# Retention and a gated FFN on one core: where the transposes of q and k, one unit's norm and the last output product stand

## The chip, the cores and the metric

The kernel runs on one core of one Trainium2 chip. The metric is the device time of one execution in microseconds (us), as a median of several runs. The core has five engines with an instruction queue each: TensorE (PE in the profile; PEld is its weight load), VectorE (DVE), ScalarE (ACT), GpSimd (POOL) and SyncE (SP), which here only issues transfers. Each engine takes its instructions in the order in which the program gives them, and waits on semaphores for the others.

## The reference

Retention over 8 batches, 8 heads, 576 positions and head size 64, followed by an RMS norm and a gated feed-forward net over the 4608 tokens that result:

```python
scores = scale * np.matmul(q, k.transpose(0, 1, 3, 2))
Dmat = np.where(rel >= 0, gamma[:, None, None] ** rel[None, :, :], 0.0)
attn = np.matmul(scores * Dmat[None], v)            # (8, 8, 576, 64)
x = attn.transpose(0, 2, 1, 3).reshape(4608, 512)
xn = x / np.sqrt(np.mean(x * x, -1, keepdims=True) + 1e-6) * rms_g
g = xn @ w_gate                                     # 512 -> 1536
out = (g * (1.0 / (1.0 + np.exp(-g))) * (xn @ w_val)) @ w_out   # 1536 -> 512
```

Everything is computed in fp32. The weights arrive as 64-bit floats and are turned into fp32 on the device, at the start.

## The kernel before

The 4608 tokens are cut into 12 *units* of 384 tokens (NU = 12, U = 384). The attention is cut into 32 *jobs* of one batch and two heads each. Units 0 and 1 are computed plainly in `start()`, while the weights are still being converted; `down(u, s)` there computes three blocks of 128 rows of a unit's output, and each copies its sums out on ACT. Between these blocks `start()` also puts the norm of unit 2 (`norm_0`: squares on ACT and their sums on DVE; `norm_1`: the mean by three small products on PE, the power -0.5 on POOL; `diagonals`; `norm_2`: one product `rb` on PE, then four scalings of `x` and four differences into `x` and `sums` on DVE), the attention's jobs 8 and 9 (`slot`), and `combine(1)`, which makes sums of blocks of `w_val` on POOL.

From unit 2 on, the two up-projections and the output projection are each done as a 2x2 block product with seven products in place of eight. Its sums of blocks are made on DVE.

`up(u, m, g)` is one *group*: m = 0 is the gate, m = 1 the value, g one of three pairs of columns. A unit has six groups, i = 0 to 5, with m = i % 2. One group is seven products of four matmuls into four PSUM banks x, y, z, w. Each bank is named for the tile, and a later product of the same group adds to it. The order, with the readers, is:

1. A11 into x; ACT copies x to `m`.
2. S2 into y; DVE: u = m + y (written `u<-m,y`).
3. S1 into z; DVE: u4 = u + z (`u<-u,z`).
4. A12 added to x; m = 0: ACT takes Silu of x; m = 1: DVE multiplies it into h (`h<-h,x`, L514).
5. S3 into w; DVE: u4 + w (`h<-u,w`, or for m = 1 `c<-u,w`, L504, then L514).
6. S4 added to z; DVE: u2 + z.
7. A22 added to w; DVE: u2 + w.

So the sixth product must wait until `u<-u,z` has read z, and the seventh until the first reader of w has read w. The generator yields after each of the seven products; yield n = 2 is the one after `u<-u,z`.

`slot(j)` puts one attention job between two groups: on PE the products of job j - 1 with v, the scores and states of job j, and the carried part of job j - 1, on DVE the weighing (`ret`, L302), the moves of the finished job into `x` (L380) and eight steps of a running sum (`sum`, L317 and L319). `SLOTS` says after which groups: for u % 3 = 0 after i = 0, 2, 4, 5; for u % 3 = 1 after 5; for u % 3 = 2 after 1, 3, 5. `behind(u, i)` calls it, and calls `prepare_next(j)` right after it: on DVE the two transposes of 32x32 blocks of the next job's q and k (`qT<-qraw`, `kT<-kraw`, L241, the *turns* of the title), on ACT four scalings of its v (L250). Then `load_next(j)` issues the loads of job j + 2 on SP. `qraw` and `kraw` have one buffer each, so these loads wait for the turns.

`across(u)` is the output projection of a unit: seven products of twelve matmuls each (L627) into xo, yo, zo, wo, with sums of h's blocks on DVE (L639). Its blocks of w_out come from DRAM through four places in SBUF; `ORDER` is the order in which they are fetched, and so of the products. After the product's third step stand the products of the next unit's `norm_1`, and after its fifth step those of `norm_2`. `result(row, col, a, ps)` adds the sums if there are any (L636), transposes 32x32 blocks into `o` on DVE (L647) and issues eight transfers to `out`: all on SP, but in the last unit the second four on ACT's queue.

The order of instructions on every engine is the order of these calls; there is no scheduler.

Of the kernel before, what the change touches and what calls it, by code (L numbers as in the profile page):

```python
# [13 lines left out]
ALU = mybir.AluOpType  # L14
# [27 lines left out]
def kernel(  # L42
# [20 lines left out]
    SQ = 32  # L63
# [510 lines left out]
        nc.sync.dma_start(out=out[u * U + s * P : u * U + s * P + P, :], in_=o)  # L574


    ORDER = (A11, S1, S3, S2, A12, S4, A22)
    DH = DM // 2
    w_blocks = dram.tile([7, P, NH, DH], F32, name="w_blocks")
    w_slots = w_out.rearrange("p f d -> p (f d)").rearrange("p (s f d) -> p s f d", s=4, d=DH)  # L580
# [32 lines left out]
    def across(u):  # L613


        h = h_of[u]
        b11, b12 = h[:, :NH, :HU], h[:, :NH, HU:]
        b21, b22 = h[:, NH:, :HU], h[:, NH:, HU:]
        t1 = ffn.tile([P, NH, HU], F32, tag="t1", name=f"t1_{u}")
        x_, y, z, w = (bank(f"{n}o_{u}") for n in "xyzw")  # L620
        s1, u2, u4 = (temp(f"{n}o_{u}") for n in ("m1", "u2", "u4"))

        def product(rhs, ps, start):
            k = 7 * (u - 2) + n_done
            for i in range(2):
                for c in range(NH):
                    nc.tensor.matmul(  # L627
                        ps[:, i * HU : i * HU + HU],
                        lhsT=w_slots[:, k % 4, c, i * P : i * P + P], rhs=rhs[:, c],
                        start=(start and i == c == 0), stop=False, skip_group_check=True,  # L630
                    )
            if n_done < 3:
                fetch()

        def add(o, a, ps):
            nc.vector.tensor_tensor(out=o, in0=a, in1=ps[:, :U], op=ALU.add)  # L636

        def block(o, a, b, op):
            nc.vector.tensor_tensor(out=o, in0=a, in1=b, op=op)  # L639

        def result(row, col, a, ps):
            r = ps[:, :U]
            if a is not None:
                r = temp(f"c{row}{col}_{u}")
                add(r, a, ps)
            o = outs.tile([P, DM], F32, tag="o", name=f"o_{u}_{row}_{col}")[:, :U]
            nc.vector.transpose(out=o, in_=r)  # L647
            o = o.rearrange("p (d t r) -> p d t r", d=2, r=SQ)
            for d in range(2):
                for i in range(P // SQ):  # L650
                    c0 = row * DH + d * P + i * SQ
                    t0 = u * U + col * HU
                    queue = nc.scalar if u == NU - 1 and d else nc.sync
                    queue.dma_start(
                        out=out[t0 : t0 + HU, c0 : c0 + SQ].rearrange("(t c) r -> c t r", c=SQ),
                        in_=o[i * SQ : i * SQ + SQ, d],
                    )

        n_done = 0
        block(t1, b12, b11, ALU.subtract)  # L660
        block(b12, b22, b12, ALU.subtract)
        yield
        product(b11, x_, True)
        nc.scalar.copy(out=s1, in_=x_[:, :U])
        block(b11, b12, b11, ALU.add)
        n_done += 1
        yield
        product(t1, z, True)
        n_done += 1
        yield  # L670
        product(b12, w, True)
        n_done += 1
        yield
        product(b11, y, True)
        add(u2, s1, y)
        add(u4, u2, z)
        result(1, 1, u4, w)
        n_done += 1
        yield
        product(b21, x_, False)  # L680
        result(0, 0, None, x_)
        block(b21, b21, b11, ALU.subtract)
        n_done += 1
        yield
        product(b22, z, False)
        result(0, 1, u2, z)
        n_done += 1
        yield
        product(b21, w, False)
        result(1, 0, u2, w)  # L690
        yield


# [137 lines left out]
    def start():  # L831

        h_of[0] = ffn.tile([P, NF, U], F32, tag="h", name="h_0")
        tables = list(zip((causal, gv, gc, gq, gx), (_causal_table(), *_decay_tables(H, D))))

        def table(i, queue):
            t, values_ = tables[i]
            src = nc.inline_tensor(values_, name=t.tensor.name + "_table")
            queue.dma_start(out=t, in_=src.ap())

        make_identity(nc, ident)
        nc.scalar.activation(out=tick, in_=mhalf[:1], func=AF.Silu)
        nc.vector.memset(ones, 1.0)
        first_places.update(find_places())
        for i in (1, 0, 2):
            table(i, nc.scalar)
        for j in range(2 * NHP):
            load_first(j)
            if j == 0:
                load_tails(0, (nc.scalar, nc.scalar, nc.sync))  # L850
            elif j == 1:
                table(3, nc.sync)
            elif j == 3:
                load_tails(1, (nc.sync,) * 3)
            load_chunks((0, 0, 1, 1, 2, 2, 2, 3)[j], nc.sync)
        table(4, nc.sync)
        nc.sync.dma_start(out=rms_g, in_=moe_rms_g.rearrange("(c p) -> p c", p=P))
        load_chunks(4, nc.sync)
        turn(0)
        scale_v(0)  # L860
        scale_v(1)
        squares = []
        for j in range(2 * NHP):
            slot(j)
            if j + 1 < 2 * NHP:
                turn(j + 1)
            if squares:
                gather(*squares.pop())
            if j + 2 < 2 * NHP:
                scale_v(j + 2)  # L870
            if j:
                u, c = divmod(j - 1, NHP)
                squares.append((u, c, square(u, c)))
            if j == 5:
                norm_1(0)
            elif j == 6:
                diagonals(0)
            weights((0, 1, 2, 2, 2, 2, 0, 0)[j])
            if j == 6:
                norm_2(0)  # L880
        gather(*squares.pop())
        load_qk(2 * NHP)
        load_kv(2 * NHP)
        for m, g in [(m, g) for g in range(NG) for m in range(2)]:
            for u in range(2):
                weights_to(4 * g + 2 * m + 1)
                for i, _ in enumerate(up_plain(u, m, g)):
                    if not (u or m or g):
                        if i == 0:
                            values(2 * NHP - 1)  # L890
                            carried(2 * NHP - 1)
                            gather(1, NHP - 1, square(1, NHP - 1))
                        elif i == 1:
                            norm_1(1)
                        elif i == 2:
                            diagonals(1)
                        elif i == 3:
                            norm_2(1)
                    weights(2)
                    if i == 1:  # L900
                        weights_to(4 * g + 2 * m + 2)
        following(2 * NHP - 1)
        weights_to(len(chunks))
        for blk, row, col in ((A11, 0, 0), (A12, 0, 1), (A22, 1, 1)):
            keep(blk, quarter(row, col))
        combine(0)
        for u in (1, 0):
            for s in range(NS):
                down(u, s)
                if u == 0:  # L910
                    (norm_0, norm_1, norm_2)[s](2)
                    if s == 1:
                        diagonals(2)
            if u:
                combine(1)
                slot(8, rest=False)
                following(8)
        slot(9)
        following(9)
# [2 lines left out]

    SLOTS = (((0, 2, 4, 5), 5), ((5,), 9), ((1, 3, 5), 10))

    def behind(u, i):
        at, n = SLOTS[u % 3]
        if i in at:
            j = u // 3 * 8 + n + at.index(i)
            slot(j)
            prepare_next(j)  # L930
            if i < 2 * NG - 1:
                load_next(j)
        if u + 1 < NU and i >= 5:
            (norm_0, norm_1, norm_2)[i - 5](u + 1)
            if i == 6:
                diagonals(u + 1)

    with tc.manual_schedule():
        start()
        for u in range(2, NU):  # L940
            made = combine_out() if u == 2 else iter(())
            for i in range(2 * NG):
                for _ in up(u, i % 2, i // 2):
                    next(made, None)
                if u > 2 and i in (1, 3):
                    fetch()
                    fetch()
                if i == 2 * NG - 1:
                    rest = across(u)
                    next(rest)  # L950
                behind(u, i)
            for i, _ in enumerate(rest):
                if i == 2:
                    behind(u, 6)
                    at, n = SLOTS[u % 3]
                    if 2 * NG - 1 in at:
                        load_next(u // 3 * 8 + n + len(at) - 1)
                elif i == 4:
                    behind(u, 7)
# [27 lines left out]
```

## Time and profile before

| | |
|---|---|
| time, median of 3 runs | 1177.43 us (1175.32 to 1178.03) |
| span of the profiled execution | 1173.6 us |
| granted TensorE clock, mean | 0.995 |
| PE busy | 1134.3 us, 97% |
| DVE busy | 692.0 us, 59% |
| ACT busy | 248.7 us, 21% |
| the turns (L241), DVE | 24 of q at 772 ns, 24 of k at 735 ns |
| transposes of results (L647), DVE, 128x384 | 40, at 578 and 583 ns |
| issue of one transfer to `out` | 439 ns median; 1.6 us median to landing |

A row of the list of waits reads: who waited (engine, tile, line), for whom, then us in all, how many times, and the longest. A row of the timeline reads: start in us from the span's start, how long, engine, line, operation, tiles written and read, their form, how many instructions are merged, and in brackets how long the engine had stood idle and what ended that. PE's ends are modelled, so that one product's end can lie 0.16 us beyond the start of the next; starts are compared here. Seven products of a group that are held up by nothing start 1.30 us apart, and those of `across` 3.90 us apart.

### The profile page before, as it was taken

The page shows a single profiled execution, that of the slowest core. Times are in us where ns is not written, and L with a number is a line of the kernel's source. Part 1 is how long each engine was busy: PE and PEld are TensorE (multiplying, and loading weights), DVE is VectorE, ACT ScalarE, POOL GpSimd, SP SyncE. Part 2 cuts the span into 40 slices and gives each one's busy share as a digit, 9 for nine tenths or more (in the row PEclk, how much of TensorE's full clock was granted, in tenths as well). Part 3 has the DMA queues.
Part 4 walks back from the last instruction along what each step waited for, and adds up shares of the span by engine and source line. Part 5 has one row for each costly group of instructions (what it writes and reads, how often), then busy time and mean ns, then how long its engine had stood idle before and what let it go on. Part 6 is the DMA issues. An engine that isn't in the chain of part 4 may idle for free.

```text
span 1173.6 us, 24291 instructions
## 1 busy us (share of the span) xinstructions
PE 1134.3 (97%) x10320; PEld 1024.2 (87%) x10320; DVE 692.0 (59%) x1410; ACT 248.7 (21%) x484; POOL 46.4 (4%) x74
## 2 busy tenths in 40 slices
PE   6689999998999999999999999999999999999998
PEld 5655555448999999999999999999999999999998
DVE  4688874018766675465675676356567566446352
ACT  5446641102111120121120211120220110120110
POOL 0000005410000000000000000000000000000000
PEclk9899999999999999999999999999999999999999
DMA  9744421422764546216426356306435412403304
GB/s 213 223 112 143 140 75 48 135 58 50 235 150 58 136 128 113 107 55 129 114 67 120 96 133 135 122 2 138 101 98 130 110 58 88 129 1 94 122 1 108
DMA packets 282364, 125.37 MB, mean 107 GB/s; under 512 B 257168, under 2 KB 264848, under 8 KB 282256
## 3 DMA queue, kind: packets, MB, share of 16 engines
q1 hardware_dynamic: 271584, 108.45, 37.2%
q10 hardware_dynamic: 10672, 15.38, 4.1%
q8 instruction: 81, 1.33, 0.5%
q14 instruction: 27, 0.22, 0.1%
HBM read 108.83 MB, written 14.94 MB: 105 GB/s over the span
## 4 chain that ended last, share of the span: by engine, by line
PE 83%; DVE 12%; issue 2%; DMA 2%; ACT 1%; DVEq 0%; SPq 0%; POOL 0%; POOLq 0%; ACTq 0%
PE z L497 12%; PE w L497 12%; PE x L497 10%; PE up L554 8%; PE xo L627 7%; PE wo L627 7%; PE zo L627 7%; PE out L568 5%; PE y L497 5%; PE yo L627 3%; DVE sum L319 3%; DVE x L380 2%; PE av L341 2%; PE s L270 2%; PE s L290 1%
## 5 line engine op out<-in xcount | busy, mean ns | idle before, releaser
L521 ACT COPY m<-x 128x384 f32<-128x384 f32 x60 | 28.8, 479 | 419.0 <-PE x L497 394.2
L497 PE MATMUL z<-x,w_gate 128*128 128x192 f32 x480 | 88.6, 328 | 6.6 <-DVE u L504 5.3
L497 PE MATMUL z<-x,w_val 128*128 128x192 f32 x480 | 88.6, 328 | 3.3 <-DVE u L504 3.3
L497 PE MATMUL x<-x,w_val 128*128 128x192 f32 x480 | 88.8, 328 | 0.0
L497 PE MATMUL x<-x,w_gate 128*128 128x192 f32 x480 | 88.5, 328 | 0.0
L497 PE MATMUL w<-sums,w_val 128*128 128x192 f32 x480 | 87.8, 326 | 0.0
L497 PE MATMUL w<-sums,w_gate 128*128 128x192 f32 x480 | 87.8, 326 | 0.0
L497 PEld LDWEIGHTS z<-x,w_gate 128*128 128x128 f32 x480 | 79.2, 190 | 8.9 <-DVE u L504 7.4
L497 PEld LDWEIGHTS z<-x,w_val 128*128 128x128 f32 x480 | 79.2, 190 | 5.7 <-DVE u L504 5.7
L627 PE MATMUL xo<-h,w_out 128*128 128x192 f32 x480 | 82.1, 328 | 0.0
L627 PE MATMUL wo<-h,w_out 128*128 128x192 f32 x480 | 81.3, 326 | 0.0
L497 PEld LDWEIGHTS x<-x,w_val 128*128 128x128 f32 x480 | 79.2, 190 | 0.6
L497 PEld LDWEIGHTS x<-x,w_gate 128*128 128x128 f32 x480 | 79.3, 190 | 0.5
L497 PEld LDWEIGHTS w<-sums,w_val 128*128 128x128 f32 x480 | 79.6, 190 | 0.0
L497 PEld LDWEIGHTS w<-sums,w_gate 128*128 128x128 f32 x480 | 79.6, 190 | 0.0
L627 PEld LDWEIGHTS xo<-h,w_out 128*128 128x128 f32 x480 | 78.1, 190 | 0.5
L627 PEld LDWEIGHTS wo<-h,w_out 128*128 128x128 f32 x480 | 78.5, 190 | 0.0
L504 DVE TENSOR_TENSOR u<-m,y 128x384 f32<-128x384 f32 x60 | 32.7, 546 | 77.5 <-PE y L497 77.5
L504 DVE TENSOR_TENSOR h<-u,w 128x384 f32<-128x384 f32 x60 | 33.2, 554 | 69.3 <-PE w L497 68.7
L302 DVE SCALAR_TENSOR_TENSOR ret<-s,causal 128x320 f32<-128x320 f32 x64 | 28.4, 484 | 67.6 <-PE last L290 41.7
L516 ACT ACTIVATE h<-h 128x384 f32<-128x384 f32 x90 | 47.1, 523 | 95.8 <-DVE h L504 95.8
L554 PE MATMUL up<-x,w_val 128*128 128x384 f32 x192 | 62.7, 487 | 2.4 <-ACT w_val L562 2.4
(151 smaller groups left out, 1779.2 us busy)
## 6 DMA issues: line engine op xcount, KB each, us to landing
w_out<-w_blocks SPq DMA_DIRECT2D x70, 768.0 KB, 5.3
out_dram<-o SPq DMA_DIRECT2D x304, 24.0 KB, 1.6
qraw<-in_q_dram SPq DMA_DIRECT2D x96, 72.0 KB, 2.6
kraw<-in_k_dram SPq DMA_DIRECT2D x96, 72.0 KB, 2.6
k<-in_k_dram SPq DMA_DIRECT2D x48, 128.0 KB, 3.0
v<-in_v_dram SPq DMA_DIRECT2D x48, 128.0 KB, 3.4
w_blocks<-w_out SPq DMA_DIRECT2D x7, 768.0 KB, 7.0
w_out<-in_moe_w_gate_dram ACTq DMA_DIRECT2D x4, 1024.0 KB, 5.2
```

What stands on the lines that cost most here:

```text
L270: nc.tensor.matmul(s[side(odd), e, i * L : i * L + L], lhsT=d["kT"][side(e), c * L : c * L + L], rhs=d["qT"][side(e), c * L : c * L + L], ...
L302: nc.vector.scalar_tensor_tensor(out=ret[:, e], in0=s[:, e, :SC].rearrange("p (c k) -> p c k", k=L), scalar=float(_gamma(H)[2 * hp + e] ** ...
L319: nc.vector.scalar_tensor_tensor(out=t[:, c], in0=t[:, c - 1], scalar=gc[:, hp : hp + 1], in1=part, op0=ALU.mult, op1=ALU.add,)
L341: mm = nc.tensor.matmul(av[odd][column(j, odd, e), i * L : i * L + L], lhsT=d["v"][side(odd), i, e] if c < NC - 1 else d["vt"][:, e], rhs= ...
L380: nc.vector.tensor_tensor(out=x[to, first - c0 // L :: 2], in0=av[odd][at, i * L : (i + n) * L].rearrange("p (c k) -> p c k", k=L), in1=g. ...
L497: nc.tensor.matmul(ps[:, i * HU : i * HU + HU], lhsT=w_up[m][:, 2 * blk + c, cut], rhs=t_of[u][blk][:, c], start=(start and i == c == 0), ...
L504: nc.vector.tensor_tensor(out=o, in0=a, in1=pairs_of(ps), op=ALU.add)
L516: nc.scalar.activation(out=o, in_=c, func=AF.Silu)
L521: nc.scalar.copy(out=s1, in_=pairs_of(x_))
L554: nc.tensor.matmul(ps[:, :U], lhsT=w_up[m][:, 4 * half + c, i * P : i * P + P], rhs=x_of[u][:, c], start=(c == 0), stop=(c == NHP - 1),)
L568: nc.tensor.matmul(ps[:, :DM], lhsT=h_of[u][:, f, s * P : s * P + P], rhs=w_out[:, f], start=(f == 0), stop=(f == NF - 1),)
L627: nc.tensor.matmul(ps[:, i * HU : i * HU + HU], lhsT=w_slots[:, k % 4, c, i * P : i * P + P], rhs=rhs[:, c], start=(start and i == c == 0) ...
```

## The change

It has three parts.

- *Turns behind the sums of the next group.* `behind` no longer calls `prepare_next(j)`; it notes j in `turns`. In the next group the turns and the scalings of v are put behind yield n = 2, which is behind `u<-u,z`. After a slot at i = 5 they stand in `across`, behind its first product and the sum of blocks after it.
- *Unit 2's norm among unit 1's outs.* `start()` computes the rows of unit 1 first and then those of unit 0. `norm_0`, `norm_1`, `diagonals` and `norm_2` of unit 2 move from unit 0's rows to unit 1's.
- *The output's product without a sum last.* In `across` the product A12 x b21, whose result needs no addition after it, moves from fifth to last. The difference b21 - b11 goes into the free tile `t1` in place of b21 itself, and stands behind the first result. In the last unit each result is transposed in two halves, and the transfers of each half alternate between the queues of SP and ACT.

```diff
-    ORDER = (A11, S1, S3, S2, A12, S4, A22)
+    ORDER = (A11, S1, S3, S2, S4, A22, A12)
...
-            nc.vector.transpose(out=o, in_=r)
-            o = o.rearrange("p (d t r) -> p d t r", d=2, r=SQ)
+            end = u == NU - 1
+            if not end:
+                nc.vector.transpose(out=o, in_=r)
+            o_of = o.rearrange("p (d t r) -> p d t r", d=2, r=SQ)
             for d in range(2):
+                if end:
+                    half = slice(d * HU, d * HU + HU)
+                    nc.vector.transpose(out=o[:, half], in_=r[:, half])
                 for i in range(P // SQ):
...
-                    queue = nc.scalar if u == NU - 1 and d else nc.sync
+                    queue = nc.scalar if end and i % 2 else nc.sync
...
         result(1, 1, u4, w)
-        n_done += 1
-        yield
-        product(b21, x_, False)
-        result(0, 0, None, x_)
-        block(b21, b21, b11, ALU.subtract)
+        block(t1, b21, b11, ALU.subtract)
         n_done += 1
         yield
         product(b22, z, False)
         result(0, 1, u2, z)
         n_done += 1
         yield
-        product(b21, w, False)
+        product(t1, w, False)
         result(1, 0, u2, w)
+        n_done += 1
+        yield
+        product(b21, x_, False)
+        result(0, 0, None, x_)
         yield
...
                 down(u, s)
-                if u == 0:
+                if u == 1:
                     (norm_0, norm_1, norm_2)[s](2)
...
             slot(j)
-            prepare_next(j)
+            turns.append(j)
             if i < 2 * NG - 1:
                 load_next(j)
...
-                for _ in up(u, i % 2, i // 2):
+                for n, _ in enumerate(up(u, i % 2, i // 2)):
                     next(made, None)
+                    if n == 2 and turns:
+                        prepare_next(turns.pop())
...
             for i, _ in enumerate(rest):
+                if i == 0 and turns:
+                    prepare_next(turns.pop())
```

## The prediction

> **What bounds the kernel now.** I read the page's busy times first, then the list of waits for PE alone, then the timeline around each of those waits.
>
> ```profile
> PE 1134.3 (97%) x10320; PEld 1024.2 (87%) x10320; DVE 692.0 (59%) x1410; ACT 248.7 (21%) x484; POOL 46.4 (4%) x74
> ```
>
> PE is the bound: 97% of the span. No part of the change takes a product away, so all it can give is in PE's waits and in the tail behind its last product. The list of PE's waits has these rows that the change touches:
>
> ```profile
> PE z L497 <- DVE u L504: 8.6, 15, 1.6
> ...
> PE z L497 <- DVE x L380: 1.2, 1, 1.2
> ...
> PE y L497 <- DVE sums L477: 0.3, 1, 0.3
> ```
>
> Fifteen times the sixth product of a group waits for `u<-u,z`. In the timeline these are the groups just after a slot whose job has a successor to turn. One with m = 0, in unit 5 (SP, weight loads and ACT left out):
>
> ```profile
> 569.44 0.28 DVE L319 SCALAR_TENSOR_TENSOR sum<-sum,gc,last 128x64 f32<-128x64 f32 x1
> 569.64 0.77 DVE L241 STREAM_TRANSPOSE qT<-qraw 128x576 f32<-128x576 f32 x1
> ...
> 570.22 1.46 PE L497 MATMUL w<-sums,w_gate 128*128 128x192 f32 x8
> 570.34 0.74 DVE L241 STREAM_TRANSPOSE kT<-kraw 128x576 f32<-128x576 f32 x1
> ...
> 571.00 0.52 DVE L504 TENSOR_TENSOR u<-m,y 128x384 f32<-128x384 f32 x1
> 571.62 0.56 DVE L504 TENSOR_TENSOR u<-u,z 128x384 f32<-128x384 f32 x1
> ...
> 572.23 1.57 PE L497 MATMUL z<-x,w_gate 128*128 128x192 f32 x8 [0.54 <-DVE u L504]
> 572.27 0.56 DVE L504 TENSOR_TENSOR h<-u,w 128x384 f32<-128x384 f32 x1
> ...
> 573.63 1.46 PE L497 MATMUL w<-sums,w_gate 128*128 128x192 f32 x8
> ```
>
> The reader is to see that y and z have long been ready; both sums stand behind the turns in DVE's queue. The z product was due at 570.22 + 1.30 = 571.52 and starts at 572.23, and the next follows after 1.40 and not 1.30: the wait costs 0.71 + 0.10 = 0.81 us, not only the 0.54 in the brackets. So the cost is the bracket + 0.27.
>
> The one slot without a turn after it (job 31, m = 1, unit 9) shows what the same place does without turns:
>
> ```profile
> 967.86 0.28 DVE L319 SCALAR_TENSOR_TENSOR sum<-sum,gc,last 128x64 f32<-128x64 f32 x1
> 968.05 0.55 DVE L504 TENSOR_TENSOR u<-m,y 128x384 f32<-128x384 f32 x1
> ...
> 968.70 0.55 DVE L504 TENSOR_TENSOR u<-u,z 128x384 f32<-128x384 f32 x1
> ...
> 970.06 1.46 PE L497 MATMUL z<-x,w_val 128*128 128x192 f32 x8
> ```
>
> There z is read by 969.25, 0.8 us before the product at 970.06, which waits for nothing.
>
> **What the Trainium skill says.** "PSUM — Partial Sum Buffer", section "Engine vs sequencer instructions": the queues of ScalarE and VectorE are strict FIFO. The extract above agrees: ready sums wait behind 1.36 us of turns. The same page, "The four PSUM rules": the chip allows a synchronised read of a partial sum in the middle of an accumulation group. Products 6 and 7 live by that, so each needs its read finished first; the 0.54 us wait shows it for z. "DMA: Bandwidth & Descriptors", section "Issuing engines are not separate DMA queues": issuing from several engines saves issue time alone. Here one issue to `out` is 439 ns, so only the issues are counted below.
>
> **The turns, part by part.** Nothing is removed: 21 pairs change place, the others stay in `start()`. Behind a slot at i = 5 the pair goes into `across`, behind the first product and the sum after it; no PE wait stands there before, and the next reader, `r<-ms`, comes more than a product (3.9 us) later. I cost these at nothing. 14 of the 15 waits belong to pairs that move; the one at 277.47 us belongs to `following(9)`, which keeps its place.
>
> The new wait is the question. What is now queued behind the turns is the first read of w, and product 7 waits for that read.
>
> *m = 0.* From the extract: the sums now start at 569.64 and 570.29 (0.65 between the two, as 968.05 to 968.70), the turns at 570.77 and 571.47 (0.48 and 0.70 between starts), and `h<-u,w` at 572.13 (0.66), ending at 572.69. Without a wait on z, product 7 is due at 570.22 + 2.60 = 572.82; waiters start about 0.05 after the release, so it is free by 572.74. The margin is 0.08 us: no wait. Five groups (in units 2, 5 and 8, idle 0.54 each) save 0.81: 4.05 us.
>
> *m = 0 in unit 2, first slot* (idle 1.01 at 299.38): here `combine_out` puts 0.4 us sums between all of these. By the same steps, with one of those sums before each of the group's own, `h<-u,w` ends near 300.46 where product 7 is due at 299.51. That makes a wait of about 1.1 where 1.28 was lost: 0.17 us saved.
>
> *m = 1.* Here one more operation, `h<-h,x`, stands between the turns and the first read of w. From a wait of this kind in unit 3:
>
> ```profile
> 380.43 1.46 PE L497 MATMUL w<-sums,w_val 128*128 128x192 f32 x8
> ...
> 382.31 1.57 PE L497 MATMUL z<-x,w_val 128*128 128x192 f32 x8 [0.41 <-DVE u L504]
> ```
>
> Before: 0.41 + 0.27 = 0.68 lost. After: the sums start at 379.73 and 380.38, the turns at 380.86 and 381.56, `h<-h,x` at 382.22, `c<-u,w` at 382.68 (0.46 on) to 383.23, so product 7 starts at 383.28 where it is due at 383.03. It loses 0.25 + 0.10 = 0.35, and 0.33 of the 0.68 is saved. Eight such groups (three each in units 3 and 6, two in 9): 2.64 us.
>
> Turns in sum: 4.05 + 0.17 + 2.64 = 6.86 us.
>
> ACT's scalings of v move with the turns: four of 0.50 and 0.34 us, 1.7 in all, in the gap between the copy of x and the first Silu, which is 3.42 us at this place (m = 0), or in m = 1 before nothing urgent. Hidden. The loads on SP that wait for the turns start 1.2 us later, against 20 us to their next use or, between slots at i = 4 and 5, some 3 us. Hidden.
>
> **Unit 2's norm.** Before, its last DVE work (four scalings, 2.19 us, and four differences) stood between the last rows of unit 0 and unit 2's first group, ahead of job 9's weighing. The group shows it:
>
> ```profile
> 271.68 1.54 PE L497 MATMUL z<-x,w_gate 128*128 128x192 f32 x8 [1.22 <-DVE x L380]
> 277.47 1.57 PE L497 MATMUL z<-x,w_gate 128*128 128x192 f32 x8 [1.65 <-DVE u L504]
> ```
>
> From the group's first product (267.01) to its sixth it takes 10.46 us. The group after the next slot has the same turns, the same sums of `combine_out`, and no norm: 291.61 to 299.38, 7.77 us. The first becomes like it: 2.69 us saved. In its new place the norm lies beside unit 1's rows, 10.3 us of products each, and what follows on PE until unit 2 is unit 0's 31 us, which needs nothing of it. On POOL the power now stands ahead of `combine(1)`, whose first sums began at 216.70 and must now wait until about 222; all end near 238 as before, 40 us ahead of their use. Hidden.
>
> **The last product.** Inside `across` the order changes, but not the number of products. The difference into `t1` must be ready for product 6. After the fourth product ends, DVE does three sums and a transpose, and with the starts 1156.85, 1157.44, 1158.03, 1158.62 of the last unit `t1` would start at 1159.13 (transposes followed at once take 0.51) and end at 1160.48. In units 2 to 10 product 6 starts 3.90 + 0.51 (`rb`) after the fourth's end at 1156.58, so at 1160.99: no wait. In the last unit there is no `rb`, and the transpose comes in two halves. A half is not in the trace. It is bounded by 0.29 (half of 0.58) and 0.58; from 576 columns in 0.77 and 384 in 0.58 it is a fixed 0.19 and 1 ns a column, so 0.38, starts 0.31 apart. I take that. `t1` ends at 1160.59, product 6 was due at 1160.48: 0.26 us lost with the restart.
>
> The tail: before, after the last product's end at 1168.46 come 0.58 of sum, 0.58 of transpose, and four issues on each queue, the last starting at 1171.1. After: half a transpose to +0.40, two issues on each queue, the second half done by +0.71, and the last issue at about +0.40 + 3 x 0.44 = +1.72 instead of +2.54: 0.82 saved, 0.56 net.
>
> **Sum.** 6.86 + 2.69 + 0.56 = 10.1 us: 1177.4 - 10.1 = 1167.3 us.
>
> **The rivals.**
> - *No wait on w.* If DVE's starts close up by 0.25 us in m = 1, the 0.35 vanish eight times (2.8) and 1167.3 becomes 1164.5. For it: the margins are tenths. Against it: every interval used is from the trace.
> - *The wait moves whole.* The m = 1 groups save nothing (2.64 back) and the m = 0 groups miss their 0.08 margin and save half (2.0 back): 1171.9. For it: FIFO, and product 7 right behind.
> - *The output's new order pays it back.* If something holds the result's transpose (its buffer's transfers are waited for there), `t1` is late in all ten units. With 1.5 us of delay, the longest idle before that transpose, less the margin of 0.46, ten units lose 1.04 + 0.10 each, 11.4 in all: 1178.7, no change. Against it: three buffers, and 8 us between a buffer's uses.
> - *Slower.* The same, and the turns' wait moved whole as well: 1178.7 + 4.6 = 1183.3. Nothing in the profile asks for it.
>
> **How the numbers follow.** 0.62 for the forecast, 0.13 for no wait, 0.17 for the wait moved whole, 0.05 and 0.03 for the last two. Faster by over 0.2% (below 1175.1) takes in the first three: 0.92; same 0.05; slower 0.03. The range is from the second case, with 0.7 us for the runs' own spread, to the third: 1163.8 to 1171.9.
>
> **What would show it.** Right: no wait of the sixth product for `u<-u,z` in units 3 to 9; in its place about eight waits of w for `c<-u,w` with idle near 0.1 us; unit 2's first group without waits for `sums` or `x`; the last issue 1.7 us behind PE's end. Wrong: waits of the wo product for `t1` in every unit, waits of w in m = 0 groups, or PE's waits on DVE in sum as large as before.

## The result, and the profile after

| | before | after |
|---|---|---|
| time, median | 1177.53 us (1175.32 to 1178.03, 4 runs) | 1185.90 us (1185.56 to 1187.21, 4 runs) |
| ratio to before, 95% interval | | 1.0077 [1.0059, 1.0094] |
| span of the profiled execution | 1173.6 us | 1184.3 us |
| from unit 2's first product to the end of PE's last | 901.43 us | 911.69 us |

The changed kernel is slower by 8.4 us where 10.1 us less were forecast. The last row of the table is used for all kernels below; it is the *stretch*. A stretch is read from the one execution of a kernel that was profiled, from PE's timeline (unit 2's first product into x starts at 267.01 before and 268.19 after; the last product ends at 1168.44 and 1179.88). It leaves out the tail, and the start, whose end differs by up to 5 us between kernels that have the same start (265.80 to 270.75).

The page's busy times of the changed kernel, called *after* from here on:

```profile
PE 1140.2 (96%) x10320; PEld 1028.6 (87%) x10320; DVE 696.1 (59%) x1414; ACT 248.3 (21%) x484; POOL 47.2 (4%) x74
```

PE has the same 10320 products. The list of PE's waits from 250 us on of after (waiting engine and tile, for whom, us in all, times, longest), to be held against the three rows of before in the prediction:

```profile
PE zo L627 <- DVE u4o L636: 13.1, 10, 1.3
PE av L360 <- issue: 2.3, 1, 2.3
PE z L497 <- DVE u L504: 1.0, 1, 1.0
PE w L497 <- DVE h L504: 0.8, 1, 0.8
```

Of the fifteen waits of z for `u`, the fourteen that the change was to remove are gone; the one left has job 10's turns ahead of it, which kept their place. The wait of w for `h` (0.84 us, unit 2) is the one of about 1.1 with its restart that the prediction worked out. At the top stands a wait that before did not have at all: in each of the ten units the second product into zo waits 1.3 us for `u4o`. The timeline of after in unit 2's `across` shows how it comes about (rows of DVE and PE; `ms` and `r` left out):

```profile
345.20 4.15 PE L627 MATMUL yo<-h,w_out 128*128 128x192 f32 x24
...
349.45 0.56 DVE L636 TENSOR_TENSOR u2o<-m1o,yo 128x384 f32<-128x384 f32 x1 [2.26 <-PE yo L627]
350.04 0.55 DVE L636 TENSOR_TENSOR u4o<-u2o,zo 128x384 f32<-128x384 f32 x1
350.63 0.55 DVE L636 TENSOR_TENSOR c<-u4o,wo 128x384 f32<-128x384 f32 x1
350.65 4.17 PE L627 MATMUL zo<-h,w_out 128*128 128x192 f32 x24 [1.31 <-DVE u4o L636]
...
355.30 4.06 PE L627 MATMUL wo<-t,w_out 128*128 128x192 f32 x24
```

The same place before:

```profile
347.36 4.15 PE L627 MATMUL yo<-h,w_out 128*128 128x192 f32 x24
...
351.35 4.06 PE L627 MATMUL xo<-h,w_out 128*128 128x192 f32 x24
...
352.21 0.55 DVE L636 TENSOR_TENSOR u4o<-u2o,zo 128x384 f32<-128x384 f32 x1
...
355.89 4.06 PE L627 MATMUL zo<-h,w_out 128*128 128x192 f32 x24
```

The second product into zo adds to what `u4o<-u2o,zo` still has to read, and that sum needs `u2o`, which needs the end of yo's product. Before, the product into xo ran in this time: the read was over at 352.76, and zo's product came at 355.89. After, nothing stands between. From yo's start to the next product's it takes 5.45 us in place of 3.99, and from zo's start over `rb` to wo's 4.65, where before such a step with `rb` took 4.54 (351.35 to 355.89), so the wait costs 1.46 + 0.11 = 1.57 us. Ten units lose 15.7 us.

The parts that were forecast to gain did so. An m = 0 group in unit 5 of after (rows of the sums and turns, and of products 5 to 7):

```profile
571.70 1.46 PE L497 MATMUL w<-sums,w_gate 128*128 128x192 f32 x8
571.77 0.55 DVE L504 TENSOR_TENSOR u<-u,z 128x384 f32<-128x384 f32 x1
572.24 0.77 DVE L241 STREAM_TRANSPOSE qT<-qraw 128x576 f32<-128x576 f32 x1
572.94 0.73 DVE L241 STREAM_TRANSPOSE kT<-kraw 128x576 f32<-128x576 f32 x1
573.00 1.46 PE L497 MATMUL z<-x,w_gate 128*128 128x192 f32 x8
573.60 0.51 DVE L504 TENSOR_TENSOR h<-u,w 128x384 f32<-128x384 f32 x1
574.30 1.46 PE L497 MATMUL w<-sums,w_gate 128*128 128x192 f32 x8
```

The products start 1.30 us apart, and w has been read at 574.11, 0.19 us before product 7 is due (0.08 were forecast). In m = 1, one operation stands between the turns and the first read of w. Unit 3 of after:

```profile
381.14 1.46 PE L497 MATMUL z<-x,w_val 128*128 128x192 f32 x8
381.61 0.52 DVE L514 TENSOR_TENSOR h<-h,x 128x384 f32<-128x384 f32 x1
382.05 0.54 DVE L504 TENSOR_TENSOR c<-u,w 128x384 f32<-128x384 f32 x1
...
382.65 1.57 PE L497 MATMUL w<-sums,w_val 128*128 128x192 f32 x8
```

Product 7 starts 1.51 after product 6, not 1.30, and itself takes 0.10 longer: 0.31 us lost where 0.35 were forecast.

The account of the stretch: 15.7 lost at zo and 3.9 at a stop of PE in unit 9 (2.29 of idle time and 1.6 of slow products behind it, below), 9.4 gained by the turns and the norm (6.76 and 2.61 in the experiments): +10.2, where 911.69 - 901.43 is +10.26.

### The profile page after: what moved, and what is told of

Same layout as the page of the kernel before. It is cut to its first block, busy times and chain, and to the rows that moved or that the text cites. A ratio compares the mean times of both kernels' runs of the same rounds, so it can differ in the third digit from the quotient of the medians.

```text
span 1184.3 us, 24297 instructions
## 1 busy us (share of the span) xinstructions
PE 1140.2 (96%) x10320; PEld 1028.6 (87%) x10320; DVE 696.1 (59%) x1414; ACT 248.3 (21%) x484; POOL 47.2 (4%) x74
## 4 chain that ended last, share of the span: by engine, by line
PE 89%; DVE 5%; DMA 2%; ACT 1%; issue 1%; SPq 0%; DVEq 0%; POOL 0%; POOLq 0%; ACTq 0%
PE w L497 13%; PE x L497 13%; PE z L497 13%; PE up L554 8%; PE zo L627 7%; PE wo L627 7%; PE y L497 6%; PE xo L627 6%; PE out L568 5%; PE yo L627 3%; PE av L341 2%; PE s L270 2%; PE s L290 1%; PE av L360 1%; DVE sum L319 1%
## 5 line engine op out<-in xcount | busy, mean ns | idle before, releaser
L554 PE MATMUL up<-x,w_gate 128*128 128x384 f32 x192 | 63.2, 488 | 1.4 <-DVE x L466 0.7
L554 PEld LDWEIGHTS up<-x,w_val 128*128 128x128 f32 x192 | 37.2, 194 | 29.0 <-ACT w_val L562 3.0
```

The source lines that it names most:

```text
L554: nc.tensor.matmul(ps[:, :U], lhsT=w_up[m][:, 4 * half + c, i * P : i * P + P], rhs=x_of[u][:, c], start=(c == 0), stop=(c == NHP - 1),)
```

## The experiments

Theory A: the loss is the read of zo, because its second product stands directly behind the product into yo. The rival B: the turns cost more than they bring, or another part of the change does. The ratios are to before on the same chip; not all rows come from one chip, so their ratios are compared and not their times.

| kernel | time, us (runs) | ratio to before | stretch | against before's 901.43 |
|---|---|---|---|---|
| only the turns | 1168.65 (6) | 0.9931 [0.9912, 0.9950] | 894.67 | -6.76 |
| only unit 2's norm | 1173.99 (15) | 0.9974 [0.9962, 0.9985] | 898.82 | -2.61 |
| only the output's order and tail | 1193.21 (4) | 1.0136 [1.0115, 1.0156] | 918.96 | +17.53 |
| the change, z added ahead of y | 1165.95 (6) | 0.9910 [0.9893, 0.9928] | 891.98 | -9.45 |
| the change, y's product third | 1184.31 (7) | 1.0061 [1.0039, 1.0083] | 910.03 | +8.60 |
| z ahead of y, turns behind n = 4 | 1161.39 (4) | 0.9880 [0.9862, 0.9898] | 888.07 | -13.36 |
| the same, and job 10's turns moved | 1161.37 (6) | 0.9877 [0.9858, 0.9895] | 886.87 | -14.56 |
| y third, turns behind n = 4, job 10's moved | 1180.22 (19) | 1.0036 [1.0026, 1.0047] | 907.18 | +5.75 |
| the change, fetches behind groups 0 and 3 | 1183.99 (5) | 1.0067 [1.0050, 1.0084] | 908.63 | +7.20 |
| the change, all fetches behind group 0 | 1181.41 (6) | 1.0054 [1.0037, 1.0071] | 907.64 | +6.21 |

### The three parts alone

*Only the turns* is before with this part of the diff:

```diff
-            prepare_next(j)
+            turns.append(j)
...
+                    if n == 2 and turns:
+                        prepare_next(turns.pop())
...
+                if i == 0 and turns:
+                    prepare_next(turns.pop())
```

> Only the turns move; norm and output as before. If the loss of the whole change comes from the output's new order (theory A: the second product into z stands right behind the product into y and must wait until u4 has read z, 10 times 1.57 us), this gains the sum forecast for the turns, about 6.9 us: near 1170.6 us. If the loss comes from the moved turns (theory B: what they delay on DVE, ACT or SP, or where PE stops for no shown reason, as at 947 us), it is at 1180 us or above.

*Only the norm* is before with `if u == 1:` in place of `if u == 0:` in `start()`.

> Only unit 2's norm moves. Both theories: unit 2's first group loses its waits for sums and x and is 2.7 us shorter, near 1174.8 us. If the first part of the program pays it back (theory B for this part: longer rows of unit 1, a later combine), it is near 1177.5 us.

*Only the output* is before with the new `ORDER`, the new order of products and results in `across`, and the last unit's halves.

> Only the output's order and its tail change. Theory A: ten waits of the zo product for u4o, 1.3 us idle and 1.57 us lost each, 15.7 us, less about 0.7 us at the tail: near 1192.5 us. Theory B: no loss here, near 1177 us.

Measured: -6.76, -2.61 and +17.53 us of stretch. The third kernel's list of PE's waits from 250 us on has the ten waits and, as the turns stayed where they were, fourteen of the fifteen of z for u:

```profile
PE zo L627 <- DVE u4o L636: 13.0, 10, 1.3
PE z L497 <- DVE u L504: 8.3, 14, 1.6
PE av L360 <- issue: 1.8, 1, 1.8
```

Its +17.53 are ten times 1.57 and the stop of 1.83 in the last line. B falls: the turns and the norm gain what they were forecast to gain, and the output's order alone loses the 15.7. The stretch leaves out the start, inside which the norm moved; the time of the whole program settles that: with only the norm moved it is 1173.99 us beside 1176.62 for before, so the start does not pay the 2.6 us back.

### The same change with zo read earlier

The order of products stays. The sum of three terms is taken in another order, so that zo is read behind its own product and only yo behind yo's:

```diff
         product(t1, z, True)
+        add(u4, s1, z)
...
         add(u2, s1, y)
-        add(u4, u2, z)
+        add(u4, u4, y)
```

> The whole change, but z is read before the product into y ends: u4 = (m1 + z) + y in place of (m1 + y) + z, the same number of sums in the same order of products. Theory A: the wait of zo for u4o is gone, 15.7 us less than the whole change: near 1170 us. If it is the place of the product in the order itself, its bank or its weights that hold it, and not the read of z, it stays near 1186 us.

Unit 2 of this kernel:

```profile
343.41 0.52 DVE L636 TENSOR_TENSOR u4o<-m1o,zo 128x384 f32<-128x384 f32 x1
...
344.73 4.15 PE L627 MATMUL yo<-h,w_out 128*128 128x192 f32 x24
...
348.71 4.06 PE L627 MATMUL zo<-h,w_out 128*128 128x192 f32 x24
...
349.38 0.55 DVE L636 TENSOR_TENSOR u4o<-u4o,yo 128x384 f32<-128x384 f32 x1
```

zo is read by 343.93, before yo's product starts, and the second product into zo follows after 3.98 us. No wait of zo is left, and with 0.71 in the tail the stretch's -9.45 makes 10.2 us less than before. This is theory A: one operand's place in one sum is worth 15.7 us between two kernels with the same products in the same order. The other 4.0 us between their stretches (911.69 and 891.98) are a stop of PE that the kernel of this run does not have; it is taken up below.

### Another cure: y's product one place earlier

y's product comes third and the first into w fourth, so that a product stands between yo's end and zo's second. `ORDER` changes with it.

```diff
         product(t1, z, True)
...
-        product(b12, w, True)
-        n_done += 1
-        yield
         product(b11, y, True)
         add(u2, s1, y)
         add(u4, u2, z)
+        n_done += 1
+        yield
+        product(b12, w, True)
         result(1, 1, u4, w)
```

> The whole change, but the product into y comes third and the first product into w fourth, so that a product of 3.9 us stands between the end of y's product and the second product into z. A (the second z product waits for u2o and u4o because it stands directly behind y's product): no wait of zo for u4o in any unit, ten times 1.57 us gone, near 1170 to 1166 us, ratio to before 0.990 to 0.994, as with the sums taken in the other order. C (the wait is for DVE as such, because the new order packs more sums and the result's transpose there): waits move to wo for t1 or for a result and the time stays above 1177 us.

A was right on zo and wrong on the time. No wait of zo is left, but in seven of the ten units yo now waits:

```profile
PE yo L627 <- DVE h L639: 12.0, 7, 1.8
```

The timeline of its unit 2 shows on what:

```profile
339.36 4.06 PE L627 MATMUL zo<-t,w_out 128*128 128x192 f32 x24
...
343.79 1.35 DVE L639 TENSOR_TENSOR h<-h 128x1152 f32<-128x1152 f32 x1
345.05 0.77 DVE L241 STREAM_TRANSPOSE qT<-qraw 128x576 f32<-128x576 f32 x1
345.19 4.17 PE L627 MATMUL yo<-h,w_out 128*128 128x192 f32 x24 [1.78 <-DVE h L639]
```

The sum of blocks that yo's product multiplies stands in DVE's queue behind the slot's weighing, running sum and squares. With two products to pass it was in time; with one it is 1.9 us late. The distance gained behind yo was taken from the distance ahead of it. The kernel with all three repairs (y third, turns behind n = 4, job 10's turns moved) was built on this order:

> Three repairs at once: y's product third, turns behind n = 4, and the turns of job 9's successor, which the change left in their place ahead of unit 2's group, noted like the others. If the waits price as read (0.31 us eight times, 1.1 in one slot of unit 2, 1.2 in the first group of unit 2), 1161 to 1163.5 us, ratio 0.986 to 0.988. If any of them is only moved to another place, 1165 to 1168 us.

At 1180.22 us it missed both of its forecasts. Here too yo waits in seven units, and the longest waits are of this kind:

```profile
434.37 5.85 PE L627 MATMUL yo<-h,w_out 128*128 128x192 f32 x24 [2.46 <-DVE h L639]
...
440.63 1.55 PE L627 MATMUL wo<-h,w_out 128*128 128x192 f32 x8
```

The product after the wait takes 6.26 us from start to start, where yo's in unit 2 of the same kernel takes 4.59 (338.62 to 343.21, with the same `ms` behind it), although nothing holds it up. Two of the seven units show this. With 1.7 us in each, and 1.7 more of waiting for `h` than in the kernel with y third alone (13.7 and 12.0), 5.0 us go, as much as the other two repairs gain (3.91 and 1.20). The 2.85 us by which the stretch is still shorter than with y third alone are about what the shorter stop in unit 9 brings (1.20 us in place of 2.47, and no low clock behind it; see below). The section on the hardware comes back to it.

### The turns behind the first read of w

With the sums in the good order, the turns go two products later:

```diff
-                    if n == 2 and turns:
+                    if n == 4 and turns:
```

> The sums in the order z then y, and the turns behind the first read of w (n = 4) in place of behind the read of z (n = 2). A (eight groups with m = 1 lose 0.31 us each and unit 2's group about 1.1 us, because the turns stand ahead of the first read of w): these waits go and the time falls by 2.5 to 3.6 us against the same kernel with n = 2 (1165.95 us), to 1162.4 to 1163.5 us. B (the turns then stand ahead of the sums of products 6 and 7 or come too late for the scores of the next slot): new waits of PE for qT, kT or x after the next group, and the time is the same or longer, 1166 to 1169 us.

The stretch falls by 3.91 us: eight times 0.31 and 1.1 in unit 2 were expected, 3.6. In unit 3 the product after the turns, in the next group, starts on time:

```profile
376.99 0.77 DVE L241 STREAM_TRANSPOSE qT<-qraw 128x576 f32<-128x576 f32 x1
377.03 1.46 PE L497 MATMUL w<-sums,w_val 128*128 128x192 f32 x8
377.69 0.73 DVE L241 STREAM_TRANSPOSE kT<-kraw 128x576 f32<-128x576 f32 x1
378.32 1.46 PE L497 MATMUL x<-x,w_gate 128*128 128x192 f32 x8
```

Nothing that PE needs soon stands behind the turns there: the reads of products 6 and 7 come late, but the next group writes z and w again only 2.6 and 5.2 us after it starts. One wait of z for u (0.97 us, unit 2's first group) is left. Its turns are those of job 10, which `following(9)` still makes ahead of the group. The last repair notes them like the others:

```diff
-        following(9)
+        turns.append(9)
+        load_next(9)
```

> The kernel with the sums in the order z then y and the turns behind n = 4, and beside it the turns of job 10 noted like all others in place of standing ahead of unit 2's first group. A (that group's wait of z for u, 0.97 us idle, is of the turns ahead of it): the wait goes, some 1.2 us less than without (1161.39 us): 1159.5 to 1160.8 us, ratio to before 0.985 to 0.987. B (the sums of blocks on DVE in unit 2 hold that read, or the turns are now missed by the next slot): 1161 to 1162 us with the wait still there.

Its list of PE's waits from 250 us to the end has one row:

```profile
PE av L360 <- POOL tick L349: 0.3, 1, 0.3
```

The stretch is 1.20 us shorter, as expected (0.97 and 0.27 of restart). The ratios of the two kernels, 0.9877 and 0.9880, do not show it, and the median lies above its forecast; 0.1% is less than their intervals tell apart. This kernel is 1.2% faster than before, and in its profile PE waits for nothing worth naming behind the start.

### The stop of PE in unit 9

Five of the kernels, after among them, have one wait behind 250 us that names no releaser ("issue": the engine waited for nothing that the profile shows). In after:

```profile
944.62 0.56 PE L360 MATMUL av<-qT,sum 64*64 64x64 f32 x19
947.48 0.45 PE L360 MATMUL av<-qT,sum 64*64 64x64 f32 x12 [2.29 <-issue]
947.85 1.97 PE L497 MATMUL x<-x,w_val 128*128 128x192 f32 x8
949.62 2.77 PE L497 MATMUL y<-sums,w_val 128*128 128x192 f32 x8
```

The slices around it (window, summed length, busy us and instructions of PE, PEld, DVE, ACT and POOL, then the granted clock, the DMA share and GB/s):

```profile
944.00:946.00 2.00, 1.18 (x78) 1.04 (x67) 0.89 (x2) 0.20 (x1) 0.00 (x1) 1.00 1.00 411
946.00:948.00 2.00, 0.53 (x13) 0.46 (x13) 0.04 (x1) 0.00 (x0) 0.00 (x0) 1.00 0.71 289
948.00:950.00 2.00, 2.00 (x10) 2.00 (x11) 1.89 (x7) 0.14 (x1) 0.00 (x0) 0.72 0.02 9
950.00:952.00 2.00, 2.00 (x8) 2.00 (x7) 1.77 (x7) 1.62 (x5) 0.00 (x0) 0.50 0.00 0
```

All DMA engines are full there. Unit 9 is where job 32 would have been loaded; without it nothing holds SP back, and it issues the four fetches behind groups 1 and 3, 768 KB each, one after the other from 937.9 on. They fill the engines until about 947. Two kernels move them. The first splits the burst (behind groups 0 and 3), the second issues it at 922.7 (behind group 0):

```diff
-                if u > 2 and i in (1, 3):
+                if u > 2 and i == 0:
                     fetch()
                     fetch()
+                    fetch()
+                    fetch()
```

> The whole change, with the fetches of the output's blocks behind groups 0 and 3 of a unit in place of 1 and 3, so that unit 9 no longer issues four of them close together. A (the stop of PE at 947 us, with the slow products after it, comes from transfers that fill all DMA engines there): no such stop in unit 9, some 3.9 us less than the whole change: 1182 us. B (the stop is chance, or belongs to the instruction stream and not to the data): the stop is there or the time stays near 1186 us.

> The whole change, with all four fetches of a unit's blocks behind group 0, which is another burst, but one that ends before the slot in unit 9 at whose products PE stopped. A (that stop and the low clock after it come from PE's instructions not arriving while the blocks' transfers fill the DMA engines): no stop near 944 to 953 us, PE some 3.9 us sooner at the end: 1182 us; the ten waits of zo stay. A stop can then appear at the slot behind group 0 of some unit instead, 1184 to 1187 us. B (the stop has to do with the place in the program and not with the transfers): it stays at that slot and so does the time, near 1186 us.

Split, the stop shrinks from 2.29 to 0.87 us and the stretch by 3.06, where it was to vanish; moved, it is gone, and the stretch is 4.05 shorter, as forecast for that run. The same slot with the burst moved:

```profile
944.00:946.00 2.00, 2.00 (x116) 1.93 (x109) 0.76 (x3) 0.52 (x1) 0.09 (x1) 1.00 0.00 0
```

So in these traces the stop goes with the burst. They are one execution of each kernel, and it is not known that every execution has the stop: those of one kernel differ by up to 8.6 us (y third, 1178.35 to 1186.96). The burst alone is not enough: before, the turns alone and the kernels with z ahead of y have it beside the same slot with no stop. What differs between them is when one packet of PE's instructions arrives; the last section has the figures.

## Why the prediction was wrong

The step that failed is in "The last product": "Inside `across` the order changes, but not the number of products. The difference into `t1` must be ready for product 6." Only the operand of product 6 was followed there. Product 5, b22 added to zo, moved up to stand directly behind yo's product, and its own condition was not looked at: zo must have been read, by a sum that needs yo. The page of the Trainium skill that the prediction quoted, "PSUM — Partial Sum Buffer", section "The four PSUM rules", was applied to the groups of `up` and not to `across`, where the same rule holds. The term taken as 0 is 1.57 us in each of ten units.

Point by point:

- *The turns*, forecast 6.86 us, measured 6.76 alone. m = 0: no wait, as forecast. m = 1: 0.31 us left in each group for 0.35; the list of waits names none of them, the products' starts show them. Right.
- *Unit 2's norm*, forecast 2.69, measured 2.61 alone. Right.
- *The tail*, forecast 0.82. From PE's end to the span's end it was 5.17 us and is 4.41: 0.76. A transpose in two halves takes 0.65 us for both, close to the 0.71 worked out. Right within 0.1.
- *The wait for `t1`* of 0.26 in the last unit: it did not come. After, zo's own wait gives `t1` 1.57 us more time; in the kernel with z read early, wo in the last unit starts 3.90 us after zo and waits for nothing either. The estimate was too careful by tenths for that kernel, in part because its second sum starts 0.47 us behind the first (1148.03 to 1148.50) where 0.59 were reckoned.
- *The rival "the output's new order pays it back"* had the place right and the wait wrong: it blamed a late `t1` behind the result's transpose. `u4o` is ahead of that transpose, and no wait for `t1` is in the profile. Its 0.05 was too little for a part whose seven products change neighbours. That the case "slower", at 1183.3, came within 3 us of the measured 1185.90 is luck: it added this late `t1` to turns whose wait had moved whole, and neither happened.
- *The stop of 4.0 us in unit 9* was not foreseen by any case. It is two fifths of the distance to before in the stretch.

Without the failed step the sum holds: the same change with zo read earlier is 10.2 us below before, for 10.1 forecast.

## What to carry to other kernels

When products that accumulate change their order, list for each product what must be read from its bank before it and what that reader itself waits for, and put the whole chain (end of one product, two sums, start of the next) against the products that stand between. A value that is read in the middle of its accumulation should be the first term of a sum, not the last. Of two cures for a wait, take the one that frees the read; moving the product earlier shortens the time for its own operand by as much.

## What was not expected of the hardware

PE can stop for 0.9 to 2.5 us at a place where no semaphore holds it. The DMA engines need not be full at that moment: in after they are when the stop begins, but in the kernel with the burst split the last transfer of data has ended by 945.0, and PE stops at 946.20. The Trainium skill, "Runtime: NRT & Kernel Launch", section "Instruction fetch mechanics", says that each engine's instructions arrive by DMA in blocks of 16 KiB, each of 256 instructions, and that a block's boundary is mostly hidden. The trace has such a queue (packets, MB, share of the engines):

```profile
q8 instruction: 81, 1.33, 0.5%
```

These are 16 KB a packet. PE's 10320 products and 10320 weight loads would fill 81 blocks, an estimate from the page's 256. In all five kernels PE stops ahead of the 8741st to 8743rd product, and in all of them the 68th packet of this queue is late. In after it runs from 945.15 to 946.09; PE stops at 945.18 and goes on at 947.48. Over the five, the packet ends between 0.5 us before and 1.2 us behind PE's arrival at this place, the stop is the longer the later the packet, and PE goes on 1.2 to 1.5 us behind its end. In the seven kernels without the stop the same packet ends 1.5 to 4.1 us before PE comes to the 8741st product. So everything in the traces fits a PE that waits for its instructions. No run moved this packet alone, and why it is late in after and not in before, which has the same burst, is open.

A pause of PE can also cost its clock, and the pause need not be long. The granted clock after the 2.46 us wait of yo, which is for DVE and not for instructions (window, sum, busy us of the engines, then clock, DMA share, GB/s):

```profile
432.00:434.00 2.00, 0.00 (x0) 0.00 (x0) 1.90 (x3) 0.00 (x0) 0.00 (x0) 1.00 1.04 347
434.00:436.00 2.00, 1.64 (x8) 1.64 (x9) 1.66 (x3) 0.00 (x0) 0.00 (x0) 0.85 0.70 280
436.00:438.00 2.00, 2.00 (x7) 2.00 (x7) 0.00 (x0) 0.00 (x0) 0.00 (x0) 0.50 0.02 9
438.00:440.00 2.00, 2.00 (x11) 2.00 (x11) 0.00 (x0) 0.00 (x0) 0.00 (x0) 0.79 0.00 0
```

If the clock is either full or half, the last three slices hold 0.60, 2.00 and 0.84 us at half clock, 3.4 in all, which cost half as much of PE's time: 1.7 us. The price measured on top of the wait is 6.26 - 4.59 = 1.67 us. Behind the start, pauses of 2.29, 2.45, 2.46 and 2.47 us were followed by such slices, those of 0.87, 1.20, 1.31 and 1.83 us, and the other waits of yo (1.62 to 1.78), were not. After the stop in unit 9 of after it is the same price: 1.77 and 2.55 us from start to start where 1.41 and 1.30 are usual, 1.6 in all. The Trainium skill, "TensorE: Matmul & The Clock Gate", Part 1, gives the half clock after an idle window of about 3.4 us; here pauses of 2.3 us were enough. So a wait of PE has a step in its price: 1.3 us of idle time cost 1.57, 2.46 cost over 4. Where between 1.83 and 2.29 us the step lies, and whether the length alone decides, four pauses do not show.
